# Spectral layer and MLP on one core: rows of the first four units moved within the chip instead of through main memory

## The chip, the cores and the metric

The kernel runs on one core of a Trainium2 chip. The metric is the time on the device in microseconds (us), the median of several runs; less is better. The engines are TensorE (PE in the rows; PEld is its weight load), VectorE (DVE), ScalarE (ACT), GpSimd (POOL) and SyncE (SP). Transfers (DMA) are issued from the queues of SP and ACT (the hardware queues) and of POOL (the software queue).

## The reference

The input `x` is 4 batches of 3008 positions with 256 channels. Each batch goes through a real Fourier transform along the positions, a complex 256x256 product with a bias, a shrinkage towards zero and the transform back; all 12032 rows then go through an MLP with 2048 hidden channels.

```python
X = np.fft.rfft(x, axis=1)
Yr = X.real @ w_r - X.imag @ w_i + b_r
Yi = X.real @ w_i + X.imag @ w_r + b_i
Yr = np.sign(Yr) * np.maximum(np.abs(Yr) - 0.01, 0.0)     # Yi alike
y = np.fft.irfft(Yr + 1j * Yi, n=3008, axis=1).astype(np.float32)
h = y.reshape(12032, 256) @ moe_w_in
out = (h * (1.0 / (1.0 + np.exp(-h)))) @ moe_w_out
```

## The kernel before

The transform of 3008 = 47 x 64 positions is done in two stages of matrix products. The **first stage** (`s1`) takes a batch in eight pieces `g` of 4 x 256 columns: the 94 rows of a piece (47 positions, two interleaved halves) are multiplied by the table `c1` and give 96 rows, which stand for 24 residues `r`, real and imaginary part, two halves. A piece has two halves of 512 columns; ScalarE copies each from PSUM into `s1_out` (batch 0; four pieces in `s1_out0`, four in `s1_out1`), and SyncE stores it into the scratch tensor `scr1` in main memory. The store is also what turns the data round: the **second stage** (`s2`) needs, for one residue, 128 rows (part, half and the 32 positions) of 256 columns. It runs in 12 **units** `u` of two residues; `u_load` brings a unit's 256 KB from `scr1` into the tile `a` (three buffers) and its table into `t2`. Then `mix` does the complex product and the shrinkage, and `i1` the first stage of the way back. In the rows the digits of a name are left out: `s_out` is `s1_out`, `c_sb` is `c1_sb`, `t` is `t2`, `s` is the PSUM tile of `s1` or of `s2`, `scr` is a scratch tensor.

The order of the opening stretch is written out by hand, each engine runs its instructions in that order:

- TensorE: the eight pieces of batch 0 (L287 and L259), pieces 0 and 1 of batch 1 (L287), then `warm`, products of a tile of zeros whose result nobody reads (L926), then a loop `u_step(u)`: `s2(u)` (L373), `mix(u - 1)` (L404), `i1(u - 2)` (L508). In the first two steps one or two `warm` products follow `s2`.
- SyncE: a store for each piece of batch 0 (L292 for the halves of pieces 0 and 7, L297 for the rest), the two weight matrices `w_r` and `w_i` (L848), and then `u_load` for units 0, 1 and 2 (L364), with tables and biases between. `u_step(u)` issues `u_load(u + 3)`.
- GpSimd: the loads of `x` (L223, L232), later a subtraction that makes the low part of `w_i` (`w_split`, L853).

A matrix product in float32 is issued as two instructions; in the split form each factor is cut into a high and a low part (`fp32r`) and three products are added. The rest of the kernel (batches 1 to 3 and the MLP) follows the loop over units; the change does not touch it.

Of the kernel before, what the change touches and what calls it, by code (L numbers as in the profile page):

```python
# [20 lines left out]
NR = 24  # L21
# [13 lines left out]
STACKED = 2  # L35

# [30 lines left out]
def dft_tables():  # L67
# [16 lines left out]
    for h in range(2):  # L84
# [5 lines left out]
    c4[0, 1] = 0.0  # L90

# [48 lines left out]
        "c1": np.pad(c1.reshape(NP, 96), ((0, 128 - NP), (0, 0))).astype(np.float32),  # L140
# [4 lines left out]
        "c5": c5.reshape(128, 128),  # L145
    }
# [3 lines left out]
def spectral_mlp_kernel(ctx: ExitStack, tc: tile.TileContext, x, w_r, w_i, b_r, b_i, w_in, w_out, c1, c2, c3, c4, c3f, c5, out):  # L150
# [14 lines left out]
    c1_sb = tf.tile([128, 96], F32, name="c1_sb")  # L165
    c1_lo = tf.tile([128, 96], F32R, name="c1_lo")
# [8 lines left out]
    c1_hl = [cst.tile([128, 96], F32R, name="c1_hi"), c1_lo]  # L175
    shift(cst, 64)
# [88 lines left out]
    def s1_halves(b, g, late=False):  # L265
        t = x_t.pop((b, g))
        if b == 0:

            o = s1_out[g // 4][:96, g % 4 * 4 * D:(g % 4 + 1) * 4 * D]
# [5 lines left out]
        for i in range(2):  # L275
# [9 lines left out]
            else:  # L285
                k = NP if X_BUFS[8 * b + g] < 2 else 128
                nc.tensor.matmul(out=p[:96, :], lhsT=c1_sb[:k, :], rhs=h[:k, :], start=True, stop=True)  # L287
            nc.scalar.copy(o[:, i * 512:(i + 1) * 512], p[:96, :])
# [66 lines left out]
    def t2_load(b, u):  # L355
        t2 = tf.tile([128, 256], F32, tag="t2", bufs=3, name="t2")
        nc.sync.dma_start(out=t2, in_=c2[:, u * 256:(u + 1) * 256])
        t2_t[b, u] = t2

    def u_load(b, u):  # L360
# [536 lines left out]
    with tc.manual_schedule():  # L897
        first = tf.tile([128, 1], F32, tag="xs", bufs=1, name="first")
        nc.vector.memset(first, 0.0)
        nc.scalar.dma_start(out=c1_sb, in_=c1)  # L900
# [18 lines left out]
        nc.scalar.copy(c1_hl[0], c1_sb)  # L919
        nc.vector.tensor_sub(c1_hl[1], c1_sb, c1_hl[0])  # L920
# [349 lines left out]
```

## Time and profile before

| | |
|---|---|
| median of 3 runs | 1287.64 us (1286.79 to 1287.7) |
| the profiled execution: its own time | 1287.78 us |
| its span, first to last instruction | 1286.0 us (1.78 us lie outside it) |
| TensorE busy | 1279.3 us, 99% of the span |
| VectorE, ScalarE, GpSimd busy | 69%, 61%, 16% |
| granted TensorE clock, mean | 1.000 of full speed |

The profile is of one execution. A row gives start and duration in us; "idle before" names the time an engine stood still ahead of an instruction, and what released it by the trace. Of a wait for several things the last one by the trace is named; where that had long ended, it was another, often a transfer.

### The profile page before, as it was taken

The numbers are of one execution on the slowest core, as the hardware profiler recorded it, in microseconds if no ns is written. First come the engines' busy times: TensorE is split into PE (matmuls) and PEld (weight loads), VectorE is DVE, ScalarE is ACT, GpSimd is POOL, SyncE is SP. The second block draws the span as 40 slices with busy tenths as digits, with TensorE's granted clock in tenths as the row PEclk, the third lists the DMA queues.
The fourth block names the chain that finished last, engine by engine and source line by source line (L and its number), as shares of the span: only waits on it lengthen the run. The fifth ranks groups of instructions, "written<-read, shape, count | busy, mean of one in ns | idle before, by whom it ended". The sixth has DMA issues, their size and how long they took to land.

```text
span 1286.0 us, 27583 instructions
## 1 busy us (share of the span) xinstructions
PE 1279.3 (99%) x10953; PEld 1259.7 (98%) x10953; DVE 893.2 (69%) x1703; ACT 789.8 (61%) x1639; POOL 206.4 (16%) x303
## 2 busy tenths in 40 slices
PE   9999999999999999999999999999999999999998
PEld 5989999999999999999999999999999999999998
DVE  4776857878768777566658766666666666666663
ACT  5456655777666666555556666666666665666654
POOL 3001012212222221121102110211012101110200
PEclk9999999999999999999999999999999999999999
DMA  8984324554464543424220111011101110110000
GB/s 292 286 255 163 124 64 119 131 162 106 120 178 130 133 126 106 131 86 126 63 72 4 46 33 33 2 33 33 37 4 33 33 33 2 33 33 15 4 23 26
DMA packets 76581, 110.31 MB, mean 86 GB/s; under 512 B 9054, under 2 KB 54998, under 8 KB 76453
## 3 DMA queue, kind: packets, MB, share of 16 engines
q1 hardware_dynamic: 62014, 78.92, 20.7%
q0 software_dynamic: 10608, 25.49, 7.7%
q10 hardware_dynamic: 3831, 4.14, 1.0%
q8 instruction: 87, 1.43, 0.4%
q14 instruction: 41, 0.34, 0.1%
HBM read 71.03 MB, written 37.49 MB: 84 GB/s over the span
## 4 chain that ended last, share of the span: by engine, by line
PE 99%; DMA 0%; issue 0%; DVE 0%; POOL 0%; POOLq 0%
PE acc L814 40%; PE h L739 19%; PE h L653 18%; PE mix L464 6%; PE mix L404 3%; PE s L439 2%; PE i L511 2%; PE i L580 2%; PE i2e L580 2%; PE s L287 1%; PE s L330 1%; PE s L373 1%; PE i L508 1%; PE i L573 1%; PE warm L926 0%; PE s L259 0%
## 5 line engine op out<-in xcount | busy, mean ns | idle before, releaser
L814 PE MATMUL acc<-wout,gh 128*128 128x256 f32 x3008 | 539.6, 277 | 0.0
L814 PEld LDWEIGHTS acc<-wout,gh 128*128 128x128 f32 x3008 | 453.7, 188 | 1.0 <-issue 1.0
L814 PE MATMUL acc<-wout,gl 128*128 128x256 f32 x1504 | 415.7, 276 | 0.0
L814 PEld LDWEIGHTS acc<-wout,gl 128*128 128x128 f32 x1504 | 282.3, 188 | 0.0
L653 PE MATMUL h<-xt,win 128*128 128x256 f32 x2016 | 259.2, 277 | 0.0
L653 PEld LDWEIGHTS h<-xt,win 128*128 128x128 f32 x2016 | 242.4, 188 | 0.6 <-issue 0.5
L660 ACT ACTIVATE g<-h 128x512 f32<-128x512 f32 (+1 forms) x177 | 102.0, 577 | 146.3 <-PE h L653 145.7
L790 DVE TENSOR_TENSOR gl<-gp,gh 128x512 fp32r<-128x512 f32 x208 | 145.9, 701 | 24.9 <-ACT gh L789 23.9
L777 ACT ACTIVATE gp<-gp 128x256 f32<-128x256 f32 x104 | 43.4, 417 | 180.0 <-DVE gp L774 180.0
L670 DVE TENSOR_TENSOR gl<-g,gh 128x512 fp32r<-128x512 f32 (+1 forms) x177 | 117.9, 666 | 47.0 <-ACT gh L669 45.2
L789 ACT CAST gh<-gp 128x512 fp32r<-128x512 f32 x208 | 129.2, 621 | 6.6
L669 ACT CAST gh<-g 128x512 fp32r<-128x512 f32 (+1 forms) x177 | 106.1, 600 | 1.6 <-PE acc L814 0.8
L739 PE MATMUL h<-xt,win 128*128 128x256 f32 x624 | 106.1, 279 | 0.0
L779 DVE TENSOR_TENSOR gp<-h,u 128x256 f32<-128x256 f32 x104 | 44.2, 425 | 78.8 <-ACT gp L778 78.8
L483 DVE TENSOR_TENSOR y<-q,mix 64x256 f32<-64x256 f32 x144 | 60.3, 419 | 41.2 <-PE mix L464 30.6
L739 PE MATMUL h<-th,sw_h 128*128 128x256 f32 x312 | 87.4, 280 | 0.0
L739 PEld LDWEIGHTS h<-xt,win 128*128 128x128 f32 x624 | 86.4, 188 | 0.1
L739 PE MATMUL h<-th,sw_l 128*128 128x256 f32 x312 | 86.2, 276 | 0.0
L739 PE MATMUL h<-tl,sw_h 128*128 128x256 f32 x312 | 86.2, 276 | 0.0
L471 POOL TENSOR_TENSOR q<-q,bias 128x256 f32<-128x256 f32 x36 | 30.0, 834 | 335.6 <-ACT q L470 335.6
L774 DVE TENSOR_TENSOR gp<-h,u 128x256 f32<-128x256 f32 x104 | 44.2, 425 | 51.0 <-PE h L739 49.7
L788 ACT ACTIVATE gp<-gp 128x512 f32<-128x512 f32 x104 | 66.3, 638 | 0.0
(170 smaller groups left out, 2335.4 us busy)
## 6 DMA issues: line engine op xcount, KB each, us to landing
x_sb<-in_x_dram POOLq DMA_DIRECT2D x69, 188.0 KB, 4.0
a<-scr SPq DMA_DIRECT2D x48, 256.0 KB
gin<-scr SPq DMA_DIRECT2D x48, 192.0 KB
t<-in_c_dram POOLq DMA_DIRECT2D x36, 256.0 KB, 3.5
scr<-i1o SPq DMA_DIRECT2D x36, 256.0 KB
t<-in_c_dram SPq DMA_DIRECT2D x48, 128.0 KB
scr<-s1o SPq DMA_DIRECT2D x32, 192.0 KB
w<-in_moe_w_in_dram SPq DMA_DIRECT2D x8, 512.0 KB
```

Source lines behind the costliest of these rows:

```text
L464: nc.tensor.matmul(out=out, lhsT=x_[:, e, c, :], rhs=m[:, e, :], start=(n == 0), stop=(n == 5))
L483: nc.vector.tensor_tensor(out=y[64 * i:64 * i + 64, r, :], in0=q[rows, i, :], in1=pv[rows, i, :], op=op,)
L580: nc.tensor.matmul(out=p[:, o:o + NP + RR], lhsT=t[:, q:q + 128], rhs=c4_sb[:, h * (NP + RR):(h + 1) * (NP + RR)], start=(h == 0), stop=(h ...
L653: nc.tensor.matmul(out=p[:, c:c + D], lhsT=w[:, e, f * 128:(f + 1) * 128], rhs=v[:, e, c:c + D], start=(m == 0), stop=(m == 5),)
L660: nc.scalar.activation(out=g[:, q], in_=p[:, q], func=ACTF.Silu)
L669: nc.scalar.copy(gh[:, q], g[:, q])
L670: nc.vector.tensor_sub(gl[:, q], g[:, q], gh[:, q])
L739: nc.tensor.matmul(out=p, lhsT=w[j], rhs=m[k], start=(begins and n == 0), stop=(n == 2), skip_group_check=True,)
L788: nc.scalar.activation(out=v, in_=v, func=ACTF.Silu)
L789: nc.scalar.copy(h, v)
L790: nc.vector.tensor_sub(l, v, h)
L814: nc.tensor.matmul(out=a[:, r, :], lhsT=v[:, q], rhs=wout[:, f, w, :], start=(begins and m == 0 and r == 0), stop=(ends and m == 2), skip_ ...
```

## The change

Four units (`DIRECT = 4`) no longer go through `scr1`. The table of the first stage for batch 0 gets 128 columns (`c1z`) instead of 96: columns 0 to 63 are the residues of units 4 to 11, columns 64 to 95 stay zero, and the last 32 hold the residues of units 0 to 3 in an order in which the four rows of one residue stand four apart. All 128 rows are copied into `s1_out`; stores into `scr1` take the first 64. For units 0 to 3, `u_direct(u, h)` copies four rows of `s1_out[h]` (16 positions of 256 columns each) straight into 64 rows of the tile `a`, one transfer of 64 KB for each residue and each `h`, so four for a unit. GpSimd issues them, except those of unit 0 with `h = 1`, one of which ScalarE issues and one SyncE. `c2z` is the table `c2` with its rows in the order that this leaves in `a`.

Besides: pieces 0 to 3 are stored at once, the stores of pieces 4 to 7 are put off to `u_step(0)`, ahead of `s2(0)` in the program; the load of `w_r` and `w_i` moves up behind the third store; piece 1 of batch 1 moves behind `s2(0)`; `warm` shrinks from 10 to 5 products, and the ones after `s2(0)` and `s2(1)` go; the low part of `w_i` is made by VectorE; a second table `c1_sb` of 96 columns is loaded for batch 1; `t3` is loaded ahead of the next unit's `u_load`; the first load of an MLP weight stands behind `u_step(0)`'s transfers.

```diff
+DIRECT = 4
...
+    c1 = np.pad(c1.reshape(NP, 96), ((0, 128 - NP), (0, 0)))
+    c1z = np.zeros((128, 128))
+    c1z[:, :96 - 8 * DIRECT] = c1[:, 8 * DIRECT:]
+    c1z[:, 96:].reshape(128, 2, 4, DIRECT)[:] = c1[:, :8 * DIRECT].reshape(128, DIRECT, 2, 4).transpose(0, 2, 3, 1)
...
+        "c2z": c2.reshape(4, 2, 16, NR * 128).transpose(1, 0, 2, 3).reshape(128, NR * 128)[:, :DIRECT * 256].astype(np.float32),
...
-            nc.tensor.matmul(out=p[:96, :], lhsT=c1_hl[m][:K, :], rhs=hl[k][:K, :], start=(n == 0), stop=(n == 2))
+            nc.tensor.matmul(out=p, lhsT=c1_hl[m][:K, :], rhs=hl[k][:K, :], start=(n == 0), stop=(n == 2))
...
-            if b == 0 and g in (0, 7):
-                c = slice(i * 512, (i + 1) * 512)
-                nc.sync.dma_start(out=v[:, g * 4 * D:(g + 1) * 4 * D][:, c], in_=o[:, c])
             if i == 0:
                 yield
+        v = v[:, g * 4 * D:(g + 1) * 4 * D]
         if b == 0:
-            if g not in (0, 7):
-                nc.sync.dma_start(out=v[:, g * 4 * D:(g + 1) * 4 * D], in_=o)
+            v, o = v[8 * DIRECT:], o[:96 - 8 * DIRECT]
+        if b == 0 and g < 4:
+            nc.sync.dma_start(out=v, in_=o)
         else:
-            store(v[:, g * 4 * D:(g + 1) * 4 * D], o, late)
+            store(v, o, late)
...
     def u_load(b, u):
...
-        nc.sync.dma_start(out=a, in_=scr1[b][2 * u:2 * u + 2].rearrange("r p d -> p r d"))
         u_t[b, u] = (a, t2_t.pop((b, u)))
+        if b or u >= DIRECT:
+            nc.sync.dma_start(out=a, in_=scr1[b][2 * u:2 * u + 2].rearrange("r p d -> p r d"))
+
+    def u_direct(u, h, engines=(nc.gpsimd, nc.gpsimd)):
+        for r, eng in enumerate(engines):
+            q = 96 + 4 * DIRECT * r + u
+            rows = s1_out[h][q:q + 3 * DIRECT + 1:DIRECT, :].rearrange("p (j d) -> p j d", d=D)
+            eng.dma_start(out=u_t[0, u][0][64 * h:64 * h + 64, r, :], in_=rows)
...
         def u_step(u):
             if u < NU:
+                t3_load(0, u)
                 if u + 3 < NU:
                     u_load(0, u + 3)
-                t3_load(0, u)
+                    if u + 3 < DIRECT:
+                        for h in range(2):
+                            u_direct(u + 3, h)
+                        flush(4)
                 s2(0, u)
-                if u < 2:
-                    warm(zero, 2 - u)
+                if u == 0:
+                    s1(1, 1, late=True)
...
         for g in range(8):
-            s1(0, g)
+            s1(0, g, late=True)
             if g in (2, 3):
                 x_ahead()
-        w32 = [w_load(w_r), w_load(w_i)]
-        u_load(0, 0)
-        u_load(0, 1)
+            if g == 2:
+                w32 = [w_load(w_r), w_load(w_i)]
+            if g == 4:
+                for u in range(2):
+                    u_load(0, u)
+                    u_direct(u, 0)
+        u_direct(0, 1, (nc.scalar, nc.sync))
+        u_direct(1, 1)
...
         u_load(0, 2)
...
+        for h in range(2):
+            u_direct(2, h)
         s1(1, 0, late=True)
-        s1(1, 1, late=True)
-        warm(zero, 10)
         w_split(w32[0], wr, nc.vector)
-        w_split(w32[1], wi, nc.gpsimd)
+        w_split(w32[1], wi, nc.vector)
+        warm(zero, 5)
```

The order of the instructions on three engines, each from the same place. On TensorE, before: from the end of batch 0's first stage to the first `mix` (`x4` is a count; the number at the end of a name tells tiles apart; a piece has two rows, one for each half).

```order
L287 MATMUL s1_267<-x_sb2_102,c1_sb_70 96x512
L287 MATMUL s1_270<-x_sb2_102,c1_sb_70 96x512
L287 MATMUL s1_274<-x_sb1_73,c1_sb_70 96x512
L287 MATMUL s1_277<-x_sb1_73,c1_sb_70 96x512
L926 MATMUL warm_280<-zero_101 128x256 x10
L373 MATMUL s2_301<-t2_143,a_252 128x128 x4
L926 MATMUL warm_312<-zero_101 128x256 x2
L373 MATMUL s2_323<-t2_254,a_256 128x128 x4
L926 MATMUL warm_334<-zero_101 128x256
L404 MATMUL mix_338<-wr0_76,xh_306 128x256
```

And now:

```order
L296 MATMUL s1_270<-x_sb2_102,c1_sb_146 96x512
L296 MATMUL s1_273<-x_sb2_102,c1_sb_146 96x512
L941 MATMUL warm_280<-zero_101 128x256 x5
L388 MATMUL s2_299<-t2_143,a_212 128x128 x4
L296 MATMUL s1_311<-x_sb1_73,c1_sb_146 96x512
L296 MATMUL s1_314<-x_sb1_73,c1_sb_146 96x512
L388 MATMUL s2_327<-t2_215,a_217 128x128 x4
L419 MATMUL mix_340<-wr0_76,xh_304 128x256
```

Piece 1 of batch 1 (`s1_274` and `s1_277`, now `s1_311` and `s1_314`) has moved behind the first `s2`, and eight of the 13 zero products have gone.

On SyncE, before: from the first store of batch 0 to the load of unit 1's rows.

```order
L292 DMA scr1_0_87<-s1_out0_82 96x512 x2
L297 DMA scr1_0_87<-s1_out0_82 96x1024 x3
L297 DMA scr1_0_87<-s1_out1_83 96x1024 x3
L292 DMA scr1_0_87<-s1_out1_83 96x512 x2
L848 DMA ws_248<-in_w_r_dram 128x2x256
L848 DMA ws_250<-in_w_i_dram 128x2x256
L364 DMA a_252<-scr1_0_87 128x2x256
L357 DMA t2_254<-in_c2_dram 128x256
L364 DMA a_256<-scr1_0_87 128x2x256
```

And now, from the table of unit 1 to unit 4's rows; ahead of this stand the stores of pieces 0 to 2, the two weight loads and the store of piece 3.

```order
L365 DMA t2_215<-in_c2z_dram 128x256
L380 DMA a_212<-s1_out1_83 64x1x256
L1037 DMA bias_75<-in_b_r_dram 64x256
L1038 DMA bias_75<-in_b_i_dram 64x256
L365 DMA t2_262<-in_c2z_dram 128x256
L355 DMA t3f_286<-in_c3f_dram 128x256
L365 DMA t2_288<-in_c2z_dram 128x256
L216 DMA scr1_0_87<-s1_out1_83 64x1024 x4
L879 DMA w64_319<-in_moe_w_in_dram 128x1024
L355 DMA t3f_321<-in_c3f_dram 128x256
L365 DMA t2_323<-in_c2_dram 128x256
L374 DMA a_325<-scr1_0_87 128x2x256
```

Ahead of unit 0 stand four stores instead of ten, and no load from the scratch tensor; `a_212` (unit 0) waits for the last copy of piece 7 alone. The table of unit 3 (`t2_288`) takes the buffer of unit 0's and so waits for `s2(0)`; the four other stores, an MLP weight and unit 4's rows (`a_325`) are queued behind it.

On GpSimd, where before the subtraction for `w_i` followed the loads of `x`, now (from the last of those loads):

```order
L240 DMA x_sb1_73<-in_x_dram 94x1024
L380 DMA a_212<-s1_out0_82 64x1x256 x2
L380 DMA a_217<-s1_out0_82 64x1x256 x2
L380 DMA a_217<-s1_out1_83 64x1x256 x2
L380 DMA a_264<-s1_out0_82 64x1x256 x2
L380 DMA a_264<-s1_out1_83 64x1x256 x2
L380 DMA a_290<-s1_out0_82 64x1x256 x2
L380 DMA a_290<-s1_out1_83 64x1x256 x2
```

Fourteen transfers of 64 KB have been added: two for unit 0 (`a_212`) and four each for units 1 (`a_217`), 2 (`a_264`) and 3 (`a_290`, the buffer that unit 0 frees).

## Rows read from the trace of the kernel before

**Rows 1.** The page: span; busy time, share of the span and instructions of TensorE.

```profile
span 1286.0 us, 27583 instructions
...
PE 1279.3 (99%) x10953; PEld 1259.7 (98%) x10953; DVE 893.2 (69%) x1703; ACT 789.8 (61%) x1639; POOL 206.4 (16%) x303
```

**Rows 2.** Waits of TensorE, whole span: engine, line, released by; total, times, longest (us).

```profile
PE warm L926 <- DVE zero L910: 1.2, 1, 1.2
PE s L373 <- ACT wi L852: 0.8, 1, 0.8
PE s L259 <- DVE sx L283: 0.2, 1, 0.2
```

**Rows 3.** Timeline, TensorE, 15 to 43 us: start, us, engine, line, what, count, idle before.

```profile
18.54 3.81 PE L287 MATMUL s<-x_sb,c_sb 128*96 128x512 f32 x8
22.18 4.48 PE L926 MATMUL warm<-zero 128*128 128x256 f32 x20
27.50 1.13 PE L373 MATMUL s<-t,a 128*128 128x128 f32 x8 [0.84 <-ACT wi L852]
28.46 1.03 PE L926 MATMUL warm<-zero 128*128 128x256 f32 x4
29.33 1.05 PE L373 MATMUL s<-t,a 128*128 128x128 f32 x8
30.22 0.60 PE L926 MATMUL warm<-zero 128*128 128x256 f32 x2
30.47 0.59 PE L404 MATMUL mix<-wr,xh 128*128 128x256 f32 x2
...
42.58 0.61 PE L373 MATMUL s<-t,a 128*128 128x128 f32 x4
```

**Rows 4.** Timeline, ScalarE, 15 to 31.5 us.

```profile
18.57 0.58 ACT L288 COPY s_out<-s 96x512 f32<-96x512 f32 x1 [0.40 <-PE s L259]
...
25.32 0.62 ACT L852 CAST wr<-ws 128x512 fp32r<-128x512 f32 x1 [2.36 <-DMA ws<-in_w_r_dram]
26.00 0.62 ACT L852 CAST wi<-ws 128x512 fp32r<-128x512 f32 x1
28.66 0.59 ACT L379 CAST xh<-s 128x512 fp32r<-128x512 f32 x1 [2.05 <-PE s L373]
...
30.29 0.42 ACT L382 ACTIVATE xl<-xl 128x256 fp32r<-128x256 f32 x1 [0.76 <-DVE xl L381]
```

**Rows 5.** Timeline of DMA issues on SyncE, 17 to 31 us.

```profile
17.34 0.30 SPq L297 DMA_DIRECT2D scr<-s_out  x1
18.20 2.69 SPq L292 DMA_DIRECT2D scr<-s_out  x2
20.95 0.42 SPq L848 DMA_DIRECT2D ws<-in_w_r_dram  x1
...
23.94 0.37 SPq L364 DMA_DIRECT2D a<-scr  x1
```

**Rows 6.** Timeline, VectorE, 10 to 26 us.

```profile
16.61 0.43 DVE L282 CAST sx<-x_pre 128x512 fp32r<-128x512 f32 x1 [1.31 <-DMA x_pre<-in_x_dram]
...
25.97 0.69 DVE L853 TENSOR_TENSOR wr<-ws,wr 128x512 fp32r<-128x512 f32 x1 [8.20 <-ACT wr L852]
```

**Rows 7.** Windows of 5 us: busy us by engine (count), granted clock, DMA share, GB/s.

```profile
10.00:15.00 5.00, 5.00 (x19) 2.63 (x18) 3.93 (x8) 3.85 (x7) 1.88 (x4) 1.00 1.03 377
15.00:20.00 5.00, 4.96 (x15) 1.93 (x13) 1.42 (x3) 3.33 (x7) 0.00 (x0) 1.00 1.02 410
20.00:25.00 5.00, 5.00 (x20) 3.24 (x19) 0.00 (x0) 1.97 (x4) 0.00 (x0) 1.00 0.85 301
```

**Rows 8.** DMA queues, 30 to 80 us: packets, MB, share of 16 engines.

```profile
q10 hardware_dynamic: 2448, 2.36, 14.0%
```

**Rows 9.** DMA issues: destination, source, queue, count, KB each, median us to landing.

```profile
x_pre<-in_x_dram POOLq DMA_DIRECT2D x10, 188.0 KB, 5.3
...
x_sb<-in_x_dram POOLq DMA_DIRECT2D x2, 376.0 KB, 8.1
```

More of the change, by code (lines that the diff above doesn't have):

```diff
@@ L145, in dft_tables, with spectral_mlp_kernel @@
         "c5": c5.reshape(128, 128),
+        "c1z": c1z.astype(np.float32),
+        "c2z": c2.reshape(4, 2, 16, NR * 128).transpose(1, 0, 2, 3).reshape(128, NR * 128)[:, :DIRECT * 256].astype(np.float32),
     }
 @with_exitstack
-def spectral_mlp_kernel(ctx: ExitStack, tc: tile.TileContext, x, w_r, w_i, b_r, b_i, w_in, w_out, c1, c2, c3, c4, c3f, c5, out):
+def spectral_mlp_kernel(ctx: ExitStack, tc: tile.TileContext, x, w_r, w_i, b_r, b_i, w_in, w_out, c1, c2, c3, c4, c3f, c5, c1z, c2z, out):
     nc = tc.nc
@@ L174, in spectral_mlp_kernel @@
     win = []
-    c1_hl = [cst.tile([128, 96], F32R, name="c1_hi"), c1_lo]
-    shift(cst, 64)
+    c1_hl = [cst.tile([128, 128], F32R, name="c1_hi"), c1_lo]
+    shift(cst, 192)
     wout = cst.tile([128, NFF, 2, D], F32R, name="wout")
@@ L286, in s1_halves @@
                 k = NP if X_BUFS[8 * b + g] < 2 else 128
-                nc.tensor.matmul(out=p[:96, :], lhsT=c1_sb[:k, :], rhs=h[:k, :], start=True, stop=True)
-            nc.scalar.copy(o[:, i * 512:(i + 1) * 512], p[:96, :])
+                w = c1_sb if b else c1z_sb
+                nc.tensor.matmul(out=p[:w.shape[1], :], lhsT=w[:k, :], rhs=h[:k, :], start=True, stop=True)
+            nc.scalar.copy(o[:, i * 512:(i + 1) * 512], p[:o.shape[0], :])
             v = scr1[b].rearrange("r (a j) d -> (r a) (j d)", a=4)
-            if b == 0 and g in (0, 7):
-                c = slice(i * 512, (i + 1) * 512)
-                nc.sync.dma_start(out=v[:, g * 4 * D:(g + 1) * 4 * D][:, c], in_=o[:, c])
             if i == 0:
                 yield
+        v = v[:, g * 4 * D:(g + 1) * 4 * D]
         if b == 0:
-            if g not in (0, 7):
-                nc.sync.dma_start(out=v[:, g * 4 * D:(g + 1) * 4 * D], in_=o)
+            v, o = v[8 * DIRECT:], o[:96 - 8 * DIRECT]
+        if b == 0 and g < 4:
+            nc.sync.dma_start(out=v, in_=o)
         else:
-            store(v[:, g * 4 * D:(g + 1) * 4 * D], o, late)
+            store(v, o, late)
     def s1_later(g, i):
@@ L356, in t2_load @@
         t2 = tf.tile([128, 256], F32, tag="t2", bufs=3, name="t2")
-        nc.sync.dma_start(out=t2, in_=c2[:, u * 256:(u + 1) * 256])
+        nc.sync.dma_start(out=t2, in_=(c2z if b == 0 and u < DIRECT else c2)[:, u * 256:(u + 1) * 256])
         t2_t[b, u] = t2
@@ L899, in spectral_mlp_kernel @@
         nc.vector.memset(first, 0.0)
-        nc.scalar.dma_start(out=c1_sb, in_=c1)
+        nc.scalar.dma_start(out=c1z_sb, in_=c1z)
         nc.scalar.activation(out=first, in_=first, func=ACTF.Silu)
@@ L917, in spectral_mlp_kernel @@
             x_ahead()
-        nc.scalar.copy(c1_hl[0], c1_sb)
-        nc.vector.tensor_sub(c1_hl[1], c1_sb, c1_hl[0])
+        nc.scalar.copy(c1_hl[0], c1z_sb)
+        nc.vector.tensor_sub(c1_hl[1], c1z_sb, c1_hl[0])
         def warm(a, n):
@@ L1003, in spectral_mlp_kernel @@
         shift(tf, 64)
+        c1_sb = tf.tile([128, 96], F32, tag="xs", bufs=1, name="c1_sb")
+        nc.sync.dma_start(out=c1_sb, in_=c1)
         for g in range(8):
-            s1(0, g)
+            s1(0, g, late=True)
             if g in (2, 3):
                 x_ahead()
-        w32 = [w_load(w_r), w_load(w_i)]
-        u_load(0, 0)
-        u_load(0, 1)
+            if g == 2:
[6 more added lines that the diff above has]
+        u_direct(1, 1)
         nc.sync.dma_start(out=bias[0:64, 0, :], in_=b_r.unsqueeze(0).to_broadcast([64, D]))
@@ L1013, in spectral_mlp_kernel @@
         u_load(0, 2)
-        win.extend(cst.tile([128, 2, DFF], F32R, tag=f"win{i}", bufs=1, name=f"win{i}") for i in range(2))
-        weight_parts()
+        for h in range(2):
+            u_direct(2, h)
         s1(1, 0, late=True)
-        s1(1, 1, late=True)
-        warm(zero, 10)
         w_split(w32[0], wr, nc.vector)
-        w_split(w32[1], wi, nc.gpsimd)
+        w_split(w32[1], wi, nc.vector)
+        warm(zero, 5)
         for u in range(NU):
@@ L1023, in spectral_mlp_kernel @@
             if u == 0:
+                win.extend(cst.tile([128, 2, DFF], F32R, tag=f"win{i}", bufs=1, name=f"win{i}") for i in range(2))
+                weight_parts()
                 w_ahead()
```

8 lines of the change are left out of this document (4 added, 4 removed).

## The prediction

> **What bounds the kernel now.** I read the page first: TensorE is busy for 99% of the span [rows 1], so time can only come from work taken off TensorE or from its waits. The list of its waits has three entries for the whole kernel [rows 2], all in the first 28 us. After that TensorE runs without a gap, so whatever moves the first `mix` moves the end by as much, as long as no new wait appears.
>
> The timeline of TensorE shows the stretch that the change rewrites [rows 3]. Batch 0's first stage ends at 18.54; the first `mix` starts at 30.47. In these 11.93 us stand the two pieces of batch 1 (18.54 to 22.18), ten zero products (22.18 + 4.48 = 26.66), a wait of 0.84 to 27.50, `s2(0)` to 28.46, two zero products, `s2(1)` at 29.33 to 30.22, one zero product. The wait is booked to the cast of `wi`, but this ended at 26.00 + 0.62 = 26.62 [rows 4], so by the rule for such rows it was another release, and the one left is unit 0's rows. Their path: the last copy of piece 7 ends at 18.57 + 0.58 = 19.15 [rows 4]; SyncE finishes issuing its store at 20.89, the two weight loads follow, and the load of unit 0's rows is issued at 23.94, when the stores have landed [rows 5]; TensorE starts 3.56 us later [rows 3]. So 8.35 us pass between a copy and its use, filled with zero products. The zero products are cover, the trip through main memory is the bound.
>
> **TensorE's part of the change.** From 18.54 it now has one piece of batch 1, half of the eight instructions from 18.54 to 22.18: 1.82 us. Then five zero products, half of 4.48: 2.24 us. It reaches `s2(0)` at 22.60. Behind that stand `s2(0)` (27.50 to 28.46: 0.96), the other piece (1.82) and `s2(1)` (29.33 to 30.22: 0.89), so `mix(0)` starts 3.67 us after `s2(0)` [rows 3]. The data of `mix(0)` are ready before that: the last conversion of unit 0 ended at 30.29 + 0.42 = 30.71 [rows 4], 3.21 us after `s2(0)` started at 27.50. If nothing is late, `mix(0)` starts at 26.27 instead of 30.47: 4.20 us is what TensorE's queue can give.
>
> **Unit 0's rows.** The last two transfers (from ScalarE and SyncE) are issued when the last copy is done, at about 19.25. No row of this trace shows a transfer within the chip, so I bound it by the nearest, the load of unit 0's 256 KB: 3.56 us from issue to use. Of this, moving the data is small: packets of about 1 KB (2448 for 2.36 MB) took 14.0% of 16 engines for 50 us [rows 8], or 46 ns each; 256 packets over 16 engines are 0.74 us, which leaves 2.82 fixed. The two new transfers are 128 packets. Over 16 engines that is 0.37, so landed at 19.25 + 2.82 + 0.37 = 22.44, hidden behind TensorE's 22.60. But each names only four rows as its source, and both could run over the same four engines: 32 packets each, 1.47, landed at 23.54. I take the middle between 22.60 and 23.54, 23.1, since the path is like the nearest row's and only the spread is unknown. `mix(0)` then starts at 26.77, a gain of 3.70.
>
> The Trainium skill has a rule on exactly this (page "DMA: Bandwidth & Descriptors", section "Why a DMA increments its semaphore by 16 and not by 1"): the number of engines divides the slowest dimension of both sides, and a hardware queue takes the lowest-numbered ones. By that rule a source of four rows runs on four engines, the same four for both transfers, and the sum would end at the second bound, 23.54 and a gain of 3.26. No row here shows which engine moved a packet.
>
> **Unit 1.** Its last two transfers are issued by GpSimd behind the same copy, one after the other. `s2(1)` stands 2.78 us behind `s2(0)`, at 25.88. With the 5.3 us that GpSimd's 188 KB loads took in the full queue [rows 9], and half a microsecond for the first issue, they land at 25.1. Cost nothing, hidden by `s2(0)` and the piece of batch 1; with the 8.1 us of the 376 KB loads they land at 27.9 and cost 2.0.
>
> **What costs nothing, and under which cover.** 128 columns of table instead of 96: a product still streams 512 columns, and a ScalarE copy of 128 rows takes 0.59 against 0.58 for 96 [rows 4]. The low part of `wi` on VectorE: 0.69, where VectorE had stood idle for 8.20 [rows 6]. The weights: ScalarE waited 2.36 us for them until 25.32 [rows 4]; loaded eight microseconds earlier they are there, and the two casts (1.24) fit between ScalarE's copy of batch 1's piece and `s2(0)`'s result. Without that cover they would delay the conversions of unit 0, which have 3.67 - 3.21 = 0.46 us to spare.
>
> **The first stage itself.** VectorE waited 1.31 us for piece 7 of `x` [rows 6] with the transfer engines full [rows 7]. The weight loads (0.5 MB) now stand in that stretch and the stores are a third smaller (eight of 384 KB before, four of 256 KB now). At 410 GB/s 0.5 MB is 1.25 us: at worst the stage ends that much later. At best VectorE's wait goes: TensorE starts piece 7 about 0.45 earlier. I take zero.
>
> **Units 2 to 11.** Unit 2's four transfers follow unit 1's on GpSimd at half a microsecond each, issued by 22.4, needed at 29.6. Unit 3's wait for `s2(0)` (24.1), are issued by 26.1, needed at 34.2. Unit 4 is the first that reads `scr1`: behind `s2(0)` SyncE issues four stores (0.30 each [rows 5]), so by about 25.5, and an MLP weight of 512 KB. Together 1.5 MB at 301 GB/s [rows 7] are 5.2 us: landed by 30.7, unit 4's rows issued then and there 3.56 later at 34.3. `s2(4)` stood 12.11 us behind `mix(0)` (42.58 [rows 3]), now at 38.9. Slack 4.6 us, cost nothing.
>
> **The sum.** The span of 1286.0 less 3.7 is 1282.3; with the 1.78 outside it 1284.1 for the profiled execution, which stands 0.14 above the median of the runs. On the median: 1287.64 - 3.7 = 1283.9 us, 0.29% less. A measurement of this kernel can tell about 0.2%, or 2.6 us, from no change.
>
> **The rivals.**
> - *Late rows, some of the gain lost.* The transfer engines are at 102% until 20 us [rows 7]. If unit 0's rows take what the weight load took in a fuller queue (20.95 to 25.32, 4.37 us [rows 4, 5]) and the four-engine spread adds 0.73 on top, plus 1.25 for a later first stage, `s2(0)` starts at 19.25 + 4.37 + 0.73 + 1.25 = 25.6 and the gain is 30.47 - 29.27 = 1.2: 1286.4. With unit 1 at 8.1 us it is 1.7 to 2.2. For it: the missing rows of a transfer with four source rows. Against: after piece 3 the stores are put off, so the queue should be empty at 19.
> - *Unit 4 comes too late: slower.* The stores of pieces 4 to 7 are queued behind `s2(0)`, and unit 4 needs all four. TensorE would wait in front of `s2(4)`. Up to 38.9, 4.6 us later than worked out, it costs nothing; from 42.6 the gain is gone; from 45.2 the kernel is slower by 0.2%. With 8.1 us [rows 9] for the stores and as much for the rows, `s2(4)` starts at 25.5 + 16.2 = 41.7, and 0.9 of the gain is left; if the 1.5 MB also move at a third of 301 GB/s (15.0 us), at 25.5 + 15.0 + 8.1 = 48.6, which is 6.0 later than before: 1293.6. For it: the engines move at least as much in a shorter time. Against: 4.6 us of slack for the one unit that is close.
> - *No change.* The gain is real but TensorE, four microseconds ahead, meets the MLP's weights or the way back, which are limited by transfers: anything up to 1287.6. Against: those loads are issued behind work of this same stretch and move with it.
>
> **How the numbers follow.** Forecast and its variants with a gain above 2.6 us: 0.75. Late rows, or a gain lost further on, within 0.2%: 0.18. Slower through unit 4 or the like: 0.07. The low end is TensorE's own limit (4.20) and 0.45 of the first stage's wait, 1287.64 - 4.65 = 1283.0, less 0.4 for the spread of the runs shown: 1282.6. The high end reaches into the late-rows case, to its 1286.4. Faster by over 0.2%: 0.75, within: 0.18, slower: 0.07.
>
> **What would show it.** `s2(0)` starting between 22.6 and 23.6 and `mix(0)` 3.7 us later; a gap in front of `s2(0)` below a microsecond; the first stage's end still near 18.5; no wait of TensorE at `s2(1)` or `s2(4)`; clock granted 1.00 throughout, as before [rows 7]. The prediction is wrong if the transfers out of four rows take over 5 us, if the first stage ends after 20, or if a wait that was hidden shows up behind unit 3.

## The result, and the profile after

The changed kernel took 1294.89 us in the median of four executions (1290.76 to 1296.39), the kernel before 1287.51; the ratio is 1.0053, interval 1.0029 to 1.0078. It was forecast 3.7 us faster and is some 7 us slower. The profile shown here is that of the fastest of the four, 1290.76 us, so it holds less than half of the loss; the profile of a usual execution comes with the first experiment.

The page and the list of TensorE's waits (answers to [rows 1, 2]):

```profile
span 1289.0 us, 27563 instructions
...
PE 1277.5 (99%) x10937; PEld 1257.8 (98%) x10937; DVE 894.1 (69%) x1704; ACT 789.0 (61%) x1639; POOL 213.9 (17%) x316
```

```profile
PE s L388 <- DMA a<-s_out: 3.4, 1, 3.4
PE warm L941 <- DVE zero L925: 1.2, 1, 1.2
PE i L523 <- DMA t3f<-in_c3f_dram: 0.8, 1, 0.8
PE s L388 <- DMA a<-scr: 0.8, 1, 0.8
PE mix L419 <- DVE xl L396: 0.3, 1, 0.3
PE i L523 <- PE mix L419: 0.3, 1, 0.3
PE i L588 <- DMA gin<-scr: 0.2, 1, 0.2
```

Ahead of unit 0 stands a wait of 3.4 where a gap of 0.84 stood, and behind it a tail of small waits, 2.4 us in all and most of them on transfers, none of which the kernel before had. The timeline of the first stretch, all engines (answers to [rows 3 to 5]):

```profile
18.71 1.88 PE L296 MATMUL s<-x_sb,c_sb 128*96 128x512 f32 x4
...
19.52 0.68 SPq L380 DMA_DIRECT2D a<-s_out  x1
19.52 1.42 ACTq L380 DMA_DIRECT2D a<-s_out  x1
...
19.79 3.61 POOL L380 DMA_DIRECT2D a<-s_out  x6 [3.72 <-ACT s_out L297]
...
20.43 2.32 PE L941 MATMUL warm<-zero 128*128 128x256 f32 x10
...
26.14 1.13 PE L388 MATMUL s<-t,a 128*128 128x128 f32 x8 [3.40 <-DMA a<-s_out]
...
27.68 3.28 SPq L216 DMA_DIRECT2D scr<-s_out  x3
...
29.64 0.49 PE L419 MATMUL mix<-wr,xh 128*128 128x256 f32 x2
```

TensorE's own queue went as forecast: the first stage ends at 18.71, the products of batch 1 and the five zero products are done at about 22.7, and `mix(0)` stands 3.50 us behind `s2(0)`. But `s2(0)` starts at 26.14, 6.62 us behind the issue of its rows at 19.52. `mix(0)` comes 0.83 us earlier than before (30.47), not 3.70.

The windows show the engines of the transfers (columns as in [rows 7]):

```profile
15.00:20.00 5.00, 5.00 (x18) 2.83 (x17) 1.91 (x4) 3.52 (x6) 1.28 (x3) 1.00 1.08 309
20.00:22.00 2.00, 2.00 (x10) 1.58 (x9) 0.00 (x0) 1.01 (x3) 2.00 (x4) 1.00 1.05 292
22.00:24.00 2.00, 0.75 (x4) 0.32 (x2) 1.29 (x2) 1.09 (x3) 1.40 (x3) 1.00 0.97 230
24.00:26.00 2.00, 0.00 (x0) 0.00 (x0) 0.00 (x0) 0.00 (x0) 0.00 (x0) 1.00 0.89 183
26.00:28.00 2.00, 1.86 (x11) 1.35 (x12) 0.00 (x0) 0.69 (x2) 0.43 (x1) 1.00 0.18 58
28.00:30.00 2.00, 2.00 (x14) 1.50 (x13) 0.69 (x1) 1.24 (x4) 1.99 (x4) 1.00 0.46 132
```

Read the last two columns together. Up to 26 us the transfer engines are as full as before, but they move 183 to 309 GB/s where they moved up to 410 [rows 7]: full of small packets (1421 for 1.41 MB from 20 to 26 us; before, 597 for 2.05 MB from 15 to 20). From 26 to 30 they are a fifth to a half busy, since four stores and a weight stand behind `s2(0)` on SyncE. The time in which they stand idle is missing later. The chain of waits, in order of time (start, us, what), shows where it comes up:

```profile
19.52 6.49 DMA a<-s_out
...
37.86 6.99 DMA scr<-i1o
44.93 2.34 DMA a<-scr
59.33 7.15 DMA t3f<-in_c3f_dram
```

The first product of the MLP, before and now:

```profile
94.64 4.60 PE L653 MATMUL h<-xt,win 128*128 128x256 f32 x34
```

```profile
97.32 1.88 PE L668 MATMUL h<-xt,win 128*128 128x256 f32 x10
```

From `mix(0)` to this product it takes 67.68 us (29.64 to 97.32), and took 64.17 before (30.47 to 94.64). So this execution gains 0.83, loses 3.51 and is 2.7 behind at the MLP; its span is 3.0 longer.

### The profile page after: what moved, and what is told of

It is laid out like the page before. It is cut to its first block, busy times and chain, and to the rows that moved or that the text cites. A ratio compares the mean times of both kernels' runs of the same rounds, so it can differ in the third digit from the quotient of the medians.

```text
span 1289.0 us, 27563 instructions
## 1 busy us (share of the span) xinstructions
PE 1277.5 (99%) x10937; PEld 1257.8 (98%) x10937; DVE 894.1 (69%) x1704; ACT 789.0 (61%) x1639; POOL 213.9 (17%) x316
## 4 chain that ended last, share of the span: by engine, by line
PE 96%; DMA 2%; DVE 1%; ACT 0%; issue 0%; SPq 0%; ACTq 0%; DVEq 0%
PE acc L829 40%; PE h L754 19%; PE h L668 18%; PE mix L479 6%; PE s L454 2%; PE i L526 2%; PE i L595 2%; PE i2e L595 2%; PE mix L419 1%; PE s L338 1%; PE s L296 1%; DMA scr<-i1o 1%; PE i L588 1%; DMA t3f<-in_c3f_dram 1%; PE i L523 1%; DMA a<-s_out 1%
## 5 line engine op out<-in xcount | busy, mean ns | idle before, releaser
L729 POOL TENSOR_TENSOR td<-xf 128x256 f32<-128x256 f32 x13 | 12.0, 924 | 338.7 <-ACT xf L629 260.6
```

## The experiments

Theory: three losses with a remedy each. (1) Unit 0's rows take 5 us and more. (2) The idle time ahead of `s2(0)` lowers TensorE's granted clock in most executions. (3) The stores that were put off come back as a backlog. Rivals: the rows are late through one edit alone (few source rows, the weight loads, a queue), or the spread has another cause.

**The same kernel again.**

> The changed kernel once more, for a second profile and the spread. In the first profile TensorE waited 3.4 us in front of s2(0) and about 2.5 us more in units 6 to 9, and the executions lay between 1290.8 and 1296.4. Theory 'opening' (the late rows of unit 0 alone decide): the wait in front of s2(0) varies with the time, 3 us in a fast execution and 7 to 9 us in a slow one. Theory 'backlog' (the transfers put off behind s2(0) decide): the wait in front of s2(0) is again 3 to 4 us, and the difference between executions lies in the waits of units 5 to 11.

1295.02 us (1294.67 to 1295.83), ratio 1.0061 [1.0046, 1.0076]. The windows of TensorE (busy, granted clock, DMA share, GB/s) and three rows of its timeline in the profiled execution, 1294.89:

```profile
24.00:26.00 2.00, 0.08 (x1) 1.00 1.12 235
26.00:28.00 2.00, 0.60 (x4) 0.72 0.88 156
28.00:30.00 2.00, 1.60 (x5) 0.50 0.20 58
30.00:32.00 2.00, 2.00 (x4) 0.50 0.39 109
32.00:34.00 2.00, 2.00 (x9) 0.58 0.80 218
34.00:36.00 2.00, 2.00 (x20) 1.00 0.92 236
```

```profile
28.40 1.19 PE L388 MATMUL s<-t,a 128*128 128x128 f32 x4 [1.80 <-DMA a<-s_out]
29.39 3.62 PE L296 MATMUL s<-x_sb,c_sb 94*96 94x512 f32 x4
...
34.04 0.48 PE L419 MATMUL mix<-wr,xh 128*128 128x256 f32 x2
```

TensorE idles 2.58 us, does the first half of `s2(0)`, idles 1.80 more, and the granted clock is 0.50 until past 32 us, the lower of its two levels (1.2 instead of 2.4 GHz): batch 1's piece takes 3.62 where it takes 1.88 in the fastest execution. `mix(0)` starts at 34.04. Of the 4.4 us between the two executions' first `mix`, some 1.8 are the second half's later rows (28.40 against about 26.6) and the rest is this clock. The fastest execution idled 3.40 at once and kept 1.00, so the length of the gap alone does not decide it. The mean granted clock over the span is 0.996 to 0.998 in all four executions here and 0.997 in the three long ones of the first four, 0.999 in the fastest; so the spread goes with the clock, which neither theory had. From `mix(0)` to the first product of the MLP it is 67.58 us (34.04 to 101.62), no less than in the fastest execution, though `mix(0)` comes 4.4 later.

The trace also records each completion signal of a transfer. The first half of `s2(0)` needs the transfer that ScalarE issued, the second that of SyncE, and each starts 0.13 or 0.14 us behind the last signal of its transfer where TensorE waits for it. In the fastest execution SyncE's was complete at 24.18 (4.66 us behind its issue) and ScalarE's at 26.01 (6.49); in this one ScalarE's at 25.78 (6.06) and SyncE's at 28.26 (8.55). Either queue can be the late one.

**One source row for each transfer.**

```diff
             q = 96 + 4 * DIRECT * r + u
+            if eng is not nc.gpsimd:
+                for i in range(4):
+                    row = s1_out[h][q + i * DIRECT:q + i * DIRECT + 1, :].rearrange("p (j d) -> p j d", d=D)
+                    eng.dma_start(out=u_t[0, u][0][64 * h + 16 * i:64 * h + 16 * i + 16, r, :], in_=row)
+                continue
```

> Unit 0's last two transfers, of four source rows each, cut into eight of one source row, each of which can use sixteen engines (16 runs of 1 KB on both sides). Theory 'four engines': the rows land 1.5 to 3 us earlier in spite of six more issues, s2(0) starts at 23 to 24.5 instead of 26.1. Theory 'full queue': all sixteen engines are busy until 24, and s2(0) stays at 26 or later.

1294.29, ratio 1.0051 [1.0036, 1.0066]. Not earlier but later: `s2(0)` at 27.82. The timeline of the issues:

```profile
19.43 5.67 SPq L382 DMA_DIRECT2D a<-s_out  x4
19.44 4.89 ACTq L382 DMA_DIRECT2D a<-s_out  x4
```

Four issues take 5.67 and 4.89 us from first to last, though each by itself takes only 0.50 to 0.85: there are pauses between them, and SyncE's last is issued at 24.60. The first of the four, 16 KB issued when the whole 64 KB was before, were complete at 24.87 and 25.41, where the whole was at 24.18 and 26.01. So the spread over engines is not the remedy here; what it would give in emptier engines stays open.

**The weights loaded as late as before**, behind unit 1's transfers.

```diff
-            if g == 2:
-                w32 = [w_load(w_r), w_load(w_i)]
...
         u_direct(1, 1)
+        w32 = [w_load(w_r), w_load(w_i)]
```

> The loads of w_r and w_i (0.5 MB) back behind unit 0's last transfers. Theory 'full queue': 0.5 MB less ahead of unit 0's rows, s2(0) starts 1.2 to 2 us earlier, at 24 to 25; ScalarE's cast of wr then waits for the load, until about 25, which is still in time for mix(0). Theory 'four engines': s2(0) stays within half a microsecond of 26.1.

1292.47, ratio 1.0037 [1.0024, 1.0051]; `s2(0)` at 25.61, half a microsecond earlier, though the DMA share from 20 to 22 us is 0.75 at 128 GB/s. ScalarE then waits for the weights until 26.96. The result lies between the two theories: the half megabyte is a part, but not the cause by itself.

**Unit 2's rows out of the way**, held back by one buffer less.

```diff
-        a = tf.tile([128, 2, D], F32, tag="a", bufs=3, name="a")
+        a = tf.tile([128, 2, D], F32, tag="a", bufs=2, name="a")
```

> Two buffers for a unit's rows instead of three, so that the four transfers of unit 2 wait for s2(0) and do not share the engines with those of units 0 and 1. Theory 'slow transfers': 256 KB less of the software queue's transfers beside unit 0's, which land 1 us earlier or more (s2(0) at 25 or before), and the second half of s2(0) no longer waits. Theory 'full queue': s2(0) stays at 26, since other transfers fill the place. Later units have less time to load, so the time as a whole rises, to 1293 to 1300.

1295.69, ratio 1.0070 [1.0051, 1.0089]; `s2(0)` at 27.27, no earlier. Unit 2's four transfers are not the cause.

**Two `x` loads behind the rows**: those of batch 1's first two pieces behind unit 1's transfers, their products behind `s2(1)`.

```diff
-            if g in (2, 3):
-                x_ahead()
...
         u_direct(1, 1)
+        for _ in range(2):
+            x_ahead()
...
-        s1(1, 0, late=True)
...
-        warm(zero, 5)
+        warm(zero, 9)
...
-                if u == 0:
+                if u == 1:
+                    s1(1, 0, late=True)
                     s1(1, 1, late=True)
```

> The two 376 KB loads of batch 1's pieces 0 and 1 are issued on GpSimd behind the rows of units 0 and 1 instead of ahead of them, and their products stand behind s2(1), with four more zero products ahead of s2(0) in their place. Theory 'full queue': 0.75 MB less ahead of the rows in the software queue and on the engines, unit 0's rows land 2 us earlier, s2(0) at 23 to 24.5. Theory 'slow transfers' (the transfers within the chip themselves take 6 us, whatever else is under way): s2(0) stays at 25.5 or later.

1288.55, ratio 1.0012 [1.0002, 1.0021]. `s2(0)` at 24.60, 1.5 us earlier, but the product of `x` waits for it by 0.95. The windows and the timeline:

```profile
20.00:22.00 2.00, 2.00 (x11) 1.71 (x9) 0.80 (x2) 1.14 (x2) 2.00 (x4) 1.00 0.48 128
```

```profile
19.09 1.42 ACTq L380 DMA_DIRECT2D a<-s_out  x1
...
24.60 2.02 PE L388 MATMUL s<-t,a 128*128 128x128 f32 x16 [2.27 <-DMA a<-s_out]
```

The engines are half empty from 20 to 22 us, and from issue to use it is still 5.5 us. But that is ScalarE's transfer alone: by the completion signals SyncE's, of the same size and issued at the same time, was complete at 22.04, 2.95 us behind its issue, and ScalarE's at 24.47. So a transfer within the chip does not need 5 us by itself; why one of two is late stays open.

**Twelve zero products in place of five.**

```diff
-        warm(zero, 5)
+        warm(zero, 12)
```

> Twelve zero products instead of five ahead of s2(0), so that TensorE works until about 26 us, when unit 0's rows have landed in the runs so far, and cannot be granted the lower clock. Theory 'clock' (the difference between an execution of 1290.8 and those of 1294 to 1296 is the stretch at 1.2 GHz behind the idle time): mean clock 1.000 in every execution, times within 1.5 us of each other, 1289 to 1291. Theory 'landing' (the slow executions are those in which the rows land still later): times still spread over 3 us or more, from 1290 to 1295, with the wait in front of s2(0) as large as before less 3 us.

1291.89 (1290.34 to 1293.38), ratio 1.0035 [1.0022, 1.0048]. The granted clock is 1.00 in every window of the profiled execution, `mix(0)` starts at 30.21, and the 1294 to 1296 of the same kernel are gone (one of the five, 1293.38, still has a mean clock of 0.998). Between the medians it is 3.1 us. Of the 3.83 us by which `mix(0)` is earlier than in the usual execution, 2.59 lie between the second half of `s2(0)` and `mix(0)` (3.05 here, 5.64 there); that is the clock, loss (2). The other 1.24 are rows that came earlier (27.16 against 28.40). But the waits on transfers behind unit 3 are all there:

```profile
PE i L523 <- DMA t3f<-in_c3f_dram: 1.4, 1, 1.4
PE s L388 <- DMA a<-scr: 1.3, 1, 1.3
...
PE i L588 <- DMA gin<-scr: 0.9, 1, 0.9
```

**The stores issued earlier, in two ways**: at once, as each piece is done (and that of piece 7 behind unit 1's transfers), or all four behind these.

```diff
-        if b == 0 and g < 4:
+        if b == 0 and g < 7:
...
         u_direct(1, 1)
+        flush(1)
...
-                        flush(4)
```

```diff
         u_direct(1, 1)
+        flush(4)
...
-                        flush(4)
```

> Stores of pieces 4 to 6 at once and of piece 7 right behind unit 0's and 1's transfers, instead of all four behind s2(0). Theory 'backlog': the time from mix(0) to the first product of the MLP goes back from 67.7 us to the 64.2 of the kernel before, because the transfer engines no longer stand at 40% between 25 and 30 us; s2(0) starts 1 to 2 us later than the 26.1 of the changed kernel, since 0.75 MB more is ahead of unit 0's rows; in all 1288 to 1290. Theory 'opening': the waits behind unit 4 stay, s2(0) is later, so the time rises above that of the changed kernel.

> The four stores issued right behind unit 0's last rows on SyncE, not behind s2(0). Theory 'backlog': from mix(0) to the MLP 64 to 65 us instead of 67.6, as with the stores at once, and the s2(0) of the changed kernel (26 us, not 28.3), so 1 to 3 us less than the changed kernel. Theory 'transfer work' (what is lost behind unit 4 is the work of the direct transfers themselves): from mix(0) to the MLP still 66 us or more.

At once: 1291.47, ratio 1.0037 [1.0025, 1.0048]; behind the rows: 1288.06 (1286.67 to 1293.76), 1.0012 [1.0000, 1.0024]. In both, first `mix` to first MLP product is back at 65.0 us. In both profiled executions TensorE waits longer for unit 0's rows (5.4 and 5.6 us) and the clock falls to 0.50; but these are the longest executions of the two runs, 1294.19 and 1293.76. The backlog is loss (3). Undoing it alone can be paid in rows and clock, and yet it takes back the most in the median: behind the rows the ratio falls from 1.0053 or 1.0061 to 1.0012, some 5.3 to 6.3 us.

**Both remedies together**: twelve zero products, stores right behind unit 1's transfers.

> The changed kernel with twelve warm-up products in place of five, and with the four stores issued right behind unit 1's transfers: the two remedies together. Theory: three things make up the loss, late rows, the clock, and the backlog of transfers, and each has its own remedy. Then the granted clock is 1.00 throughout, first mix to first product of the MLP takes 65 us (67.6 in the changed kernel), the first mix starts at 30.5 to 32, and the time is 1286.8 to 1289, with a small spread. Rival: the stores ahead push the rows back (28.8 in the run with the stores alone), so that even twelve products do not reach, the clock falls all the same and some executions are at 1292 to 1294.

1286.82 (1284.96 to 1289.99), ratio 0.9998 [0.9989, 1.0008]. The windows and the waits of TensorE:

```profile
26.00:28.00 2.00, 0.93 (x8) 0.96 (x9) 0.00 (x0) 0.00 (x0) 0.00 (x0) 1.00 0.76 247
28.00:30.00 2.00, 2.00 (x9) 0.96 (x9) 0.69 (x1) 1.01 (x3) 1.51 (x3) 1.00 0.83 254
```

```profile
PE s L388 <- DMA a<-s_out: 1.6, 1, 1.6
PE warm L941 <- DVE zero L925: 1.2, 1, 1.2
PE s L267 <- DVE sx L291: 0.2, 1, 0.2
```

The engines are at 0.76 and 0.83 where they were at 0.18 and 0.46, the waits of the tail are gone, and first `mix` to MLP takes 63.12 us (30.56 to 93.68); with the twelve products alone it takes 68.65 (30.21 to 98.86), from nearly the same start. Against these the ratio falls by 0.37%, some 4.8 us; against the stores alone by 0.14%, some 1.8. So the shares of clock and backlog depend on which is taken away first. The two remedies take back the whole loss and nothing more: `mix(0)` starts where it did before the change.

**Is ScalarE's queue the late one?** In the changed kernel the queues' rows (packets, MB, share of 16 engines) from 22.9 to 26.2 us hold all 68 packets of q10, which has none from 17 to 22.9:

```profile
q10 hardware_dynamic: 68, 0.07, 7.0%
```

So ScalarE's transfer begins to move 3.4 us or more behind its issue. The edit, in the changed kernel and in that with two `x` loads later:

```diff
-        u_direct(0, 1, (nc.scalar, nc.sync))
+        u_direct(0, 1, (nc.sync, nc.sync))
```

> The changed kernel, with both of unit 0's last transfers issued by SyncE (two of 0.68 us one behind the other, the second done by about 20.9) in place of one by ScalarE and one by SyncE. Theory: ScalarE's queue is the late one. In the changed kernel the row of ScalarE's queue (q10) shows its packets only after 23 us, 3.5 us behind the issue at 19.52, while SyncE's queue moved all along. Then the second half's rows are there at 23.5 to 24.8, unit 0's product starts 1.5 to 2.5 us earlier than the changed kernel's 26.14, TensorE is idle for under 2 us ahead of it, its granted clock stays at 1.00, and the time is 1288.5 to 1291 (the 3.5 us behind the first mix are still lost). Rival: all engines are full until 26 us, whichever queue it is; the product starts at 25.5 or later and the time stays at 1291 to 1296.

> The kernel with the x loads of the next batch's first two pieces behind the rows, and unit 0's last transfers both issued by SyncE. Theory: ScalarE's queue is the late one here too (its packets appear from 22.0 us, 2.9 behind the issue at 19.09, in a stretch in which the engines are half idle); the product starts at 22.8 to 23.8 in place of 24.60, and since the products of the next batch's first pieces then wait longer for their x, the time is 1286 to 1287.5 (1288.55 with ScalarE's). Rival: a transfer within the chip takes 5 us on any queue; 24.3 or later and 1288 to 1289.

1294.07, ratio 1.0050 [1.0033, 1.0067], the halves of `s2(0)` at 25.90 and 28.31: that queue is not the cause in full engines, as the usual execution, with SyncE's transfer the later one, had shown. With the `x` loads later 1288.12, ratio 1.0007 [0.9997, 1.0016]: the first half starts without a wait 3.07 us behind its issue (19.71 to 22.78), the second 4.1 behind its own (20.43 to 24.53), at a DMA share of 0.20 from 20 to 22. What was won is lost again at the product of `x`, which waits 1.75.

**Unit 0 alone by direct transfers**; stores at once, both last transfers on SyncE, units 1 to 3 from the scratch.

```diff
-DIRECT = 4
+DIRECT = 1
...
-        if b == 0 and g < 4:
+        if b == 0 and g < 7:
...
-        u_direct(0, 1, (nc.scalar, nc.sync))
-        u_direct(1, 1)
+        u_direct(0, 1, (nc.sync, nc.sync))
+        flush(1)
+        u_load(0, 1)
...
-        warm(zero, 5)
+        warm(zero, 8)
```

> Only unit 0 takes its rows by transfers within the chip, both of its last ones issued by SyncE; units 1 to 3 read the scratch again as before the change, the stores of pieces 4 to 6 are issued at once and that of piece 7 behind unit 0's transfers; eight warm-up products in place of five. Theory: a transfer of unit 0 is late since twelve others of 64 KB and the loads stand with it, and the backlog comes from stores that were put off. Then unit 0's product starts at 23.3 to 25, the first mix 3 to 4 us later, unit 1's product waits under 2 us, first mix to first product of the MLP takes 64 to 65 us, and the time is 1284.5 to 1287. Rival: the stores fill the engines as they did before the change, the rows come at 26 or later or the wait moves to unit 1, whose load stands behind them, and the time is 1287.5 to 1290.

1294.38, ratio 1.0053 [1.0038, 1.0068]: a miss. The halves of `s2(0)` start at 28.79 and 30.62, over 8 us behind the issue at 20.41, although the direct transfers of the other units are gone and the DMA share from 22 to 28 us is only 0.70 to 0.77; the clock falls to 0.50. So neither the other units' transfers nor full engines are needed for late rows. Here both transfers stand on SyncE's queue among its stores; with the stores at once SyncE's stands behind one too, is issued only at 22.12 and complete at 30.09. That this is the cause was not tried by itself.

**Making room for the rows.** First the stores behind unit 2's `t2` load, with twelve products; then also one `x` load (of two) behind unit 1's transfers, its product behind `s2(1)`, with ten products; then that with SyncE for both rows.

```diff
-            if g in (2, 3):
+            if g == 2:
                 x_ahead()
...
         u_direct(1, 1)
+        x_ahead()
...
+        flush(4)
         s1(1, 0, late=True)
-        warm(zero, 5)
+        warm(zero, 10)
...
-                        flush(4)
...
-                if u == 0:
+                if u == 1:
                     s1(1, 1, late=True)
```

> The changed kernel with twelve warm-up products in place of five and with the four stores issued behind the load of unit 2's t2 tile, some 2 to 3 us after unit 0's transfers, where the run with both remedies issued them right behind those. Theory: the stores took 0.5 to 1 us from the rows there (27.07 against about 26.5 with the warm-up products alone), and the engines have room for them from 26 us. Then unit 0's product starts at 25.8 to 26.8, the first mix at 29.8 to 30.3, first mix to first product of the MLP takes 63 to 64 us, and the time is 1285.7 to 1286.7 (0.2 to 1 us below the run with both remedies, 1286.82). Rival: the rows come when they come, and stores issued later only arrive later: 27 us again, 1286.5 to 1288.

> The kernel of the run before this one, with the x load of the next batch's second piece behind unit 1's transfers, its product behind unit 1's second stage (it stood behind unit 0's), and ten warm-up products. Theory: x of two pieces (376 KB of the 4096-byte packets of the software queue) cost the rows 1.5 us in the run with both later; one piece costs half. Unit 0's product starts at 25 to 26, the first mix at 29 to 30, the product of the second piece waits under 0.5 us, and the time is 1285 to 1286.5. Rival: the x load then collides with unit 1's and unit 2's rows, and what unit 0 gains is paid at unit 1 or at that product: no change against the run before, or 0.5 to 1 us more.

> The same with both of unit 0's last transfers issued by SyncE. Theory: with the engines full, SyncE's second transfer stands behind SyncE's earlier stores just as ScalarE's stands behind others, so the start of unit 0's product moves by less than 0.5 us either way and the time with it (it was 25.90 and 28.28 for the two halves with this edit alone). Rival: ScalarE's queue starts 2.9 to 3.5 us behind its issue, SyncE's does not: 1 us earlier and 1284.5 to 1285.5.

1287.78 (ratio 1.0003 [0.9994, 1.0012]), 1285.99 (0.9991 [0.9982, 1.0000]) and 1286.35 (0.9993 [0.9984, 1.0001]). The first is the rival's result: the second half of `s2(0)` still waits, until 27.71. The second kernel, its waits and its timeline, TensorE:

```profile
PE warm L941 <- DVE zero L925: 1.2, 1, 1.2
PE s L267 <- DVE sx L291: 0.2, 1, 0.2
```

```profile
24.76 2.02 PE L388 MATMUL s<-t,a 128*128 128x128 f32 x16
26.69 1.93 PE L296 MATMUL s<-x_sb,c_sb 94*96 94x512 f32 x4
28.05 0.80 PE L419 MATMUL mix<-wr,xh 128*128 128x256 f32 x2
```

No wait on a transfer is left, and `mix(0)` is 2.4 us earlier than in the kernel before. In the median 1.3 us of that arrive at the end; this profiled execution is the fastest, 1284.80. With SyncE for both, the transfers were complete 3.1 and 3.8 us behind their issues, but in that execution the first stage ended 1.2 us later (19.60 against 18.38) and `s2(0)` started at 25.63 without a wait, so the time does not tell which queue is better.

**Fewer zero products there**, seven and five, to see when the rows land.

> The kernel with one x load later (1285.99) with seven warm-up products in place of ten, so that TensorE's own queue reaches unit 0 some 1.3 us earlier, at about 23.4. Theory: a transfer within the chip needs 4 to 5.5 us from issue to use here (19.14 to between 23.1 and 24.7), so unit 0's product starts at 23.4 to 24.4 with a wait of under 1 us, and the time is 1285.2 to 1286. Rival: the rows land just before 24.76, the wait takes the place of the products, and nothing changes: 1286 again.

> The same with five, the number of the changed kernel; TensorE reaches unit 0 at about 22.5. Theory: a wait of 1 to 2 us ahead of unit 0's product, which starts where it does with seven; a wait of that length leaves the granted clock at 1.00, so the time is that of seven within 0.5 us. Rival: the idle time lets the clock fall in some executions, and the times spread up to 1290 as they do in the changed kernel.

1285.76 (0.9993 [0.9984, 1.0002]) and 1287.34 (1.0003 [0.9994, 1.0012]). With seven the first half of `s2(0)` starts unhindered at 23.41, the rest at 24.42 (wait 0.40); with five all of it at 24.78 after 2.19 us of waiting. The rows were issued at 19.48 and 19.36: 4.9 and 5.4 us. That is the time until both are there. By the completion signals one of the two takes 3.3 us in each kernel, ScalarE's with seven products and SyncE's with five, and the other 4.8 and 5.3. Fewer products give nothing more. The expectation that five would be as fast as seven within 0.5 us missed: they are 1.6 slower. In part that is its rival, the clock: three of the eleven executions with five have a mean clock of 0.998 (1287.34 to 1288.23), none with seven is below 0.999. But two with five at 1.000 take 1287.01 and 1287.99, so the rest is not explained.

## Why the prediction was wrong, point by point

**What bounds the kernel: right.** The waits of the first 28 us decide, and the end follows the first `mix` as long as nothing new waits; here something new did. From the first product of the MLP to the end of the span the kernel before takes 1191.4 us, the fastest execution of the changed kernel 1191.7 and the usual one 1191.5.

**TensorE's part: right.** `s2(0)` reached at about 22.7 (22.60 forecast), `mix(0)` 3.50 behind it (3.67).

**Unit 0's rows: the step that failed first, a size.** "Landed at 19.25 + 2.82 + 0.37 = 22.44" or 23.54 stands against 26.14 in the fastest execution, 6.62 us behind an issue at 19.52. The 2.82 fixed were taken from a load from main memory in emptying queues. The nearest rows to a landing in full queues, 4.37 and 5.3, stood beside it and were used for a rival and for unit 1. With room made for the rows both transfers are complete 4.5 to 5.5 us behind the first issue, without it 6 to over 10. The forecast's size does occur, but for one of the two: 2.6 to 3.3 us in five of the six kernels with `x` loads later. What it missed is that the later of two transfers decides, and that full engines and queues delay either; why one starts late stays open. "After piece 3 the stores are put off, so the queue should be empty at 19" was wrong: the share stays at 0.89 to 1.05 until 26.

By the rule of the Trainium skill cited there (page "DMA: Bandwidth & Descriptors", section "Why a DMA increments its semaphore by 16 and not by 1") the sum ended at 23.54, late too, by less. The trace agrees with the number of engines: ScalarE's transfer of four source rows is 68 packets on its queue, 64 of 1 KB and four of 4 bytes, with four completion signals at the end; its four transfers of one source row are 128, 64 of them of 4 bytes, with sixteen signals each. Which engines these are no view shows. But the spread is not what made the rows late: transfers of one source row came no earlier.

**Clock "1.00 throughout": failed.** The sum had TensorE wait half a microsecond. With gaps of 2.58 and 1.80 around half of `s2(0)` it was granted 0.50 until past 32 us, which took 2.6 us there, and five products in place of twelve cost 3.1 us between the medians. No rival had it. The ten zero products of the kernel before were cover for the clock too, and the change halved them.

**Units 2 to 11, "slack 4.6 us, cost nothing": failed.** The rival *unit 4 comes too late* had the mechanism, stores behind `s2(0)`, but put it at 0.07, and in the wrong place: of the waits in the fastest execution only 0.8 is on rows from the scratch, and for unit 8; the others are on `t3f`, the way back, and what these hold up. Unit 4 itself came in time (`s2(4)` at 41.63 without a wait), though its rows were issued at 35.90 and not by 30.7: the stores, priced at 0.30 an issue, took SyncE over 1 us each (three in 3.28). The step priced the first unit behind the stores, not the transfers behind that unit, although the rival *no change* named the way back as limited by transfers. Size: 3.5 us in that execution, 4.8 between the ratios with and without the stores moved, twelve products in both. A slip in that rival's sum changes nothing: 1.5 MB at a third of 301 GB/s are 15.6 us by the step's own 5.2, not 15.0.

**The rest.** The first stage ended at 18.71 (zero taken, 0.17 measured). No wait on unit 1's rows shows in the fastest execution; `s2(1)` starts 2.69 behind `s2(0)`. The range's upper end, 1286.4, was *late rows* with one loss; here three came together.

**The sum by what was measured.** In the usual execution `mix(0)` starts at 34.04, 7.27 behind the forecast 26.77: 2.6 of that is the clock, the rest the rows. From there to the MLP it takes 67.58, 3.41 more than before. Together these are 10.7 of the 10.8 us by which its span, 1293.1, exceeds the forecast 1282.3. With clock and backlog remedied the time is 1286.82, that of no change. What was forecast beyond that needs the rows by 23; they come at about 24.5 at best while TensorE waits for nothing else, which leaves 1.3 us (0.09%, at the edge of its interval).

## What to carry to other kernels

Price a new path by the slowest comparable row in the same stretch, not by one from an emptier queue: full engines and small packets add more than bytes divided by a rate. Filler products ahead of a wait may hold up the clock, so take them out only when the wait is seen to be gone. And work put off a full queue has to be followed to the end of the stretch that is limited by transfers, not to its first user; look for windows in which the engines then stand idle.

## What the runs showed of the hardware

- A 64 KB transfer within the chip, from four source rows and issued by SyncE or ScalarE, was complete 2.6 to 5.5 us behind its issue in the six kernels with `x` loads later, 4.7 and 6.5 us in the changed kernel's fastest execution, 6.1 and 8.6 in its usual one, and 8.3 and 9.3 among SyncE's stores.
- Such a transfer reported with four completion signals, one from a single source row (16 KB in 16 runs of 1 KB) with sixteen.
- A transfer issued by ScalarE started to move 1 to 5 us behind its issue: its 68 packets first appear between 20 and 21 us in the kernel with seven products (issue 19.49), after 22.9 in the changed one (19.52) and after 24 with both remedies (19.18).
- Four issues of 16 KB in a row took SyncE 5.67 us and ScalarE 4.89 from first to last (0.50 to 0.85 each), as long as the transfers that they were to shorten.
- With a DMA share of 0.89 to 1.05 the engines moved 183 to 292 GB/s while the rows were under way (410 before): the share alone does not say how much is moved.
